# Six pairs of row blocks instead of four take seven products in the second matmul of a feed-forward beside a long convolution, with their factors in tiles that fall idle

## The chip, the cores and the metric

One Trainium2 chip, of which the kernel uses one core. The metric is the device time of one execution in microseconds (us); the time before is the median of three runs. TensorE (PE in the profile) multiplies matrices, VectorE (DVE) and ScalarE (ACT) work element by element, GpSimd (POOL) and SyncE (SP) issue DMAs here. Each engine executes its own instructions in the order in which they stand in the program, and waits where one of them needs what another engine has not yet made.

## The reference

```python
def _A_ref(q, k, v, shift_k, ssm_k, ssm_D):
    # k_shift: causal depthwise convolution of k with 4 taps
    kv = k_shift * v
    # kv_f, kf_f: FFT over the sequence, padded to 2 S
    y = irfft2(kv_f * kf_f)[:S]
    y = y + kv * ssm_D
    return q * y

def _B_ref(x, w1, w2):
    h = silu(einsum("bsd,df->bsf", x, w1))
    return einsum("bsf,fd->bsd", h, w2)

x = A_q                       # (1, 2048, 1024)
xn = _layernorm(x)
return x + _A_ref(xn, A_k, A_v, A_shift_k, A_ssm_k, A_ssm_D) + _B_ref(xn, B_w1, B_w2)
```

S is 2048 rows, D is 1024 channels, F is 3584 hidden channels. Everything is float32.

## The kernel before

**Two pieces of work side by side.** The feed-forward (GEMM1: x times w1, a SiLU; GEMM2: h times w2) is nearly all of PE's work. The convolution runs by a split Fourier transform: eight groups of 128 channels (`g` 0 to 7; the text counts them 1 to 8), each with a gate (`kin`, `acc`: taps, times v), a split into parts (`cm`, `hl`), a first stage of 48 matmuls on PE with `cfw`, additions and products on the spectrum `spec` on DVE, a split of the result into `zh` and `zl`, an inverse of 48 matmuls with `civ` on PE, and a gated result `yt`, which is added to the output. A group's `kin`, `acc` and `spec` have one buffer each, so the groups follow one another.

**Precision.** An operand is split into a high and a low float16 part (`split`: ACT makes the high one, DVE the low one), and a product is three matmuls, high x high, high x low, low x high.

**GEMM2.** The hidden channels are 28 blocks of 128, in 14 pairs (`NP`). The rows are 16 tiles (`NT`), the output columns two halves of `W` = 512. A *plain* pair adds its two blocks to each of the 32 output tiles: 32 x 2 x 3 = 192 matmuls of 512 columns. The pairs in `PAIRS` (8, 9, 12, 13) go another way: their products for 2 x 2 blocks of rows, columns and hidden channels are formed by seven products `P1` to `P7` of sums of blocks instead of eight (`PRODUCTS` names the factor of h and the factor of w2 in each). A GEMM2 tile of that kind covers four output tiles, and there are eight of them (`tiles2`), so such a pair takes 8 x 7 x 3 = 168 matmuls, of which those of the last tile's P7 and P4 are cut into 384 and 128 columns. The price is sums: `quad` makes the seven factors of h in GEMM1 (`A11` ... `S4`), and `norms_w2` the seven factors of w2 (`B11`, `T3`, `T2`, `B21`, `T1`, `B22`, `T4`), with T2 = T3 + B11 and T4 = B21 - T2, for which a tile `hold` keeps T3 and then T2.

**Order of GEMM2.** First the plain pairs: 20 blocks in `NC` = 5 chunks of 4 for each half, whose split w2 lies in the places of `W2PLACE` (`places` are eight tiles that held x during GEMM1). Then `units2`: tile after tile, in each P1, P7, P6, P2, P5, then the next tile's P1, then P3, P4. The seven w2 factors are in the places of `FPLACE` and stay there for all eight tiles. `load_h` loads h for both parts into halves of `wo`. `evacuate2` brings a tile's sums out of PSUM with ACT and DVE, and POOL adds them to the output by DMA.

**What sets the order.** The code is a set of generators (streams) that yield operations or conditions; `Order.run` picks the stream whose next operation could start first, by a table of durations, and so writes one fixed list of instructions for each engine. A change in one stream thus moves the others. Tiles are taken from rings: `places`, `wo` (six pairs of halves), `hfs` (three), `hts` (two, `ht`: staging of h in GEMM1, and of the convolution when GEMM1 is over).

Of the kernel before, what the change touches and what calls it, by code (L numbers as in the profile page):

```python
# [20 lines left out]
P = 128  # L21
# [9 lines left out]
W = 512  # L31
# [20 lines left out]
RAWS = {"B11": [(0, 0)], "B21": [(1, 0)], "B22": [(1, 1)], "T1": [(0, 1), (0, 0)], "T2": [(0, 0)],  # L52
        "T3": [(1, 1), (0, 1)], "T4": [(1, 0)]}
# [242 lines left out]
def h3_ffn_kernel(ctx, tc, x, kp, vs, fs, shift, dskip, w1, w2, cfwd, cinv, out):  # L296
# [81 lines left out]
    hsf = [{p[0]: dram.tile([4, P, NQ, 2, P], F16, name=f"hsf{p[0]}{b}") for p in PRODUCTS.values()} for b in range(2)]  # L378
# [529 lines left out]
    def quad(i, sp):  # L908

        def factors(names, hf, toks=()):  # L910
            n = len(names)
            yield hts.ready if n == 1 else hts.pairs
            ht, ttok = (hts.tile if n == 1 else hts.pair)([P, 4 * n, 2, P], F16, n)
            yield from split(ht[:, :, 0], ht[:, :, 1], hf, wsc[:, i, 2:3], toks)
            for f, name in enumerate(names):
                yield L(hsf[sp][name][:, :, PAIRS.index(i)].rearrange("q p h s -> p q (h s)"),
                        ht[:, 4 * f:4 * f + 4].rearrange("p q h s -> p q (h s)"))
                ttok.set()
# [215 lines left out]
    def feed_forward():  # L1134
# [12 lines left out]
        for h in range(2):  # L1147
            for ts in TOGETHER[h]:
                pos = {}
                for c in range(NC):  # L1150
                    for t in ts:
# [7 lines left out]
                        yield from steps2(pos[t][0], hx, wc, c == 0, c == NC - 1)  # L1159
# [14 lines left out]
    def steps2(po, hx, wc, first, last, more=False, of=range(4), q=slice(0, W)):  # L1174
        o = po[:, q]
        for n in of:
            def mm(n=n):
                kw = dict(skip_group_check=more)
                nc.tensor.matmul(o, hx[:, n, 0, :], wc[:, n, 0, q], start=first and n == 0, stop=False, **kw)  # L1179
                nc.tensor.matmul(o, hx[:, n, 0, :], wc[:, n, 1, q], start=False, stop=False, **kw)  # L1180
                nc.tensor.matmul(o, hx[:, n, 1, :], wc[:, n, 0, q], start=False, stop=last and n == 3, **kw)  # L1181
            yield T(mm, o, [hx[:, n], wc[:, n, :, q]], 3 * (size(o) / 2400 + 0.005))
# [14 lines left out]
    def units2():  # L1197

        def product2(n, u, o, first=False, of=range(4), q=slice(0, W)):
# [7 lines left out]
            htok.set()  # L1207
            if u == len(tiles2) - 1:
# [5 lines left out]
        for u in range(len(tiles2)):  # L1214
# [18 lines left out]
            if last:  # L1233
                yield from product2("P2", u, one[0], of=(0, 1))
# [6 lines left out]
            if last:  # L1241
                yield from product2("P2", u, one[0], of=(2, 3))
# [102 lines left out]
    def load_h():  # L1345
        yield flag["factors"]
        for h in range(2):
            for c, t in [(c, t) for ts in TOGETHER[h] for c in range(NC) for t in ts]:
                yield wo.ready
                flag["h", h, t, c].what = o, _ = wo.tile([P, 4, 2, P], F16)  # L1350
                yield L(o, hs[t // 4][t % 4][:, PLAIN[4 * c]:PLAIN[4 * c] + 4])
                flag["h", h, t, c].set()
        for u, n in uses2():
            sp, q = tiles2[u]
            yield wo.ready
            flag["h2", u, n].what = o, _ = wo.tile([P, NQ, 2, P], F16)
            yield L(o, hsf[sp][PRODUCTS[n][0]][q])
            flag["h2", u, n].set()
        flag["h end"].set()
# [28 lines left out]
    def norms_w2():  # L1388
# [18 lines left out]
        for h in range(2):  # L1407
            for c in range(NC):
# [5 lines left out]
                flag["w2", h, c].n = 2  # L1414
                for a in (0, 2):
                    i = PLAIN[4 * c + a] // 2
                    raw, tok = yield from next_w2()
                    add(split(wc[:, a:a + 2, 0, :], wc[:, a:a + 2, 1, :], raw, tau[:, i:i + 1], (tok, flag["w2", h, c])), 0.05)
        yield places[FPLACE[0]].ready
        hold, ktok = places[FPLACE[0]].tile([P, NQ, W], F32)  # L1420
        for k, (name, (_, of)) in enumerate(PRODUCTS.items()):
            r = places[FPLACE[k + 1]]
            yield r.ready
            wc, wtok = w2f[name] = r.tile([P, NQ, 2, W], F16)
            flag["w2f", name].n = NQ
            held = of in ("T2", "T3", "T4")
            if held:
                if of != "T3":
                    yield flag["held", before]
                flag["held", of].n = NQ  # L1430
                before = of
            for a, i in enumerate(PAIRS):
                raw, tok = yield from next_w2()
                src, toks = raw, (tok, flag["w2f", name])
                if held:
                    src, toks = hold[:, a], (flag["w2f", name], flag["held", of])
                if of == "T3":
                    b12, t12 = yield from next_w2()
                    yield v_tt(src, raw, b12, SUB)
                    tok.set()  # L1440
                    t12.set()
                elif of == "T2":
                    yield v_tt(src, src, raw, ADD)
                    tok.set()
                elif of == "T4":
                    yield v_tt(src, raw, src, SUB)
                    tok.set()
                elif of == "T1":
                    b11, t11 = yield from next_w2()
                    yield v_tt(raw, raw, b11, SUB)  # L1450
                    t11.set()
                add(split(wc[:, a, 0, :], wc[:, a, 1, :], src, tau2[:, i:i + 1], toks), 0.05)
        yield flag["held", "T4"]
        ktok.set()
# [8 lines left out]
    def load_w2():  # L1463
# [4 lines left out]
        for h, j in [(h, j) for h in range(2) for j in PLAIN[::2]]:  # L1468
# [4 lines left out]
        for _, of in PRODUCTS.values():  # L1473
            for i in PAIRS:
                for q, h in RAWS[of]:
                    yield lambda: free("ready")
                    raw, tok = free("ready")[0].tile([P, W])
                    yield L(raw, w2r[:, 2 * i + q, h * W:(h + 1) * W])
# [20 lines left out]
    def convolution(floor):  # L1499
# [13 lines left out]
        ctxs["nm"] = ps_r  # L1513
# [491 lines left out]
```

## Time and profile before

| | |
|---|---|
| three runs | 1236.89, 1237.17, 1238.01 us |
| median | 1237.17 us |
| profiled execution, first to last instruction (its span) | 1235.0 us |
| PE busy | 1225.7 us, 99% of the span |
| DVE busy | 1121.9 us, 91% |
| ACT busy | 744.0 us, 60% |
| POOL busy | 142.0 us, 12% |
| HBM traffic | 236 GB/s over the span |

The profile gives the span of one execution; its time with what lies around the span isn't listed, and the median of the runs is 2.2 us longer than the span. A row of a group reads: line, engine, operation, output <- inputs, shapes, count | busy us, mean ns of one | idle us of the engine just before, and what ended it. A row in order of time begins with its start and its length in us. Matmuls overlap in the pipeline, so their mean (377 ns for 512 columns) is more than the distance from one to the next. In the rows by stage "PEclk" is the granted clock of PE as a share of its full speed.

### The profile page before, as it was taken

What the parts mean: (1) busy time and instruction counts of PE and PEld (TensorE: products, weight loads), DVE (VectorE), ACT (ScalarE), POOL (GpSimd) and SP (SyncE); (2) the same over time, 40 slices, a digit from 0 to 9 for tenths busy, and PEclk for the clock granted to TensorE, in tenths of its full rate; (3) what the DMA queues carried; (4) which work ended last, traced back from release to release, by engine and by line L of the source; (5) the groups of instructions that cost most, each with busy time, mean ns of one, the idle gap of its engine ahead of it and who ended that gap; (6) DMA issues with size and microseconds to landing.
All of it is one profiled execution on the core that took longest, in us unless ns stands there. A gap on an engine that the chain in (4) does not pass through costs nothing.

```text
span 1235.0 us, 17269 instructions
## 1 busy us (share of the span) xinstructions
PE 1225.7 (99%) x6128; PEld 596.6 (48%) x6128; DVE 1121.9 (91%) x1366; ACT 744.0 (60%) x1299; POOL 142.0 (12%) x164
## 2 busy tenths in 40 slices
PE   9999999999999999999999999999999999999998
PEld 7645444444444444444444544544454454445445
DVE  8999996989699979998999899989979979998993
ACT  7778887877767787758653632563263264536231
POOL 2000000000000020001110300210030030113114
PEclk9999999999999999999999999999999999999999
DMA  9289889999999698968997887699596688978777
GB/s 341 78 278 312 304 298 308 286 273 335 324 359 286 218 303 278 268 213 242 345 336 184 190 257 179 155 271 259 115 216 171 134 167 247 255 161 137 164 147 103
DMA packets 254438, 293.21 MB, mean 237 GB/s; under 512 B 48784, under 2 KB 167824, under 8 KB 252176
## 3 DMA queue, kind: packets, MB, share of 16 engines
q1 hardware_dynamic: 227760, 267.46, 69.3%
q0 software_dynamic: 26592, 24.65, 15.1%
q8 instruction: 48, 0.79, 0.3%
q14 instruction: 38, 0.31, 0.1%
HBM read 193.48 MB, written 98.57 MB: 236 GB/s over the span
## 4 chain that ended last, share of the span: by engine, by line
PE 96%; DVE 2%; ACT 1%; issue 1%; DMA 1%; POOL 0%; DVEq 0%
PE ff L1179 15%; PE ff L1180 15%; PE ff L1181 15%; PE ff L1027 13%; PE ff L1028 13%; PE ff L1029 13%; PE ps L1668 2%; PE ps L1669 2%; PE ps L1670 2%; PE ft L616 1%; PE ps L1863 1%; PE ps L1861 1%; PE ps L1862 1%; DMA out<-yt 1%; PE ff L1932 1%
## 5 line engine op out<-in xcount | busy, mean ns | idle before, releaser
L1180 PE MATMUL ff<-x,wo 128*128 128x512 f16 (+2 forms) x872 | 328.5, 377 | 0.0
L1179 PE MATMUL ff<-x,wo 128*128 128x512 f16 (+2 forms) x872 | 328.4, 377 | 0.0
L1181 PE MATMUL ff<-x,wo 128*128 128x512 f16 (+2 forms) x872 | 328.4, 377 | 0.0
L1028 PE MATMUL ff<-x,wo 128*128 128x512 f16 (+2 forms) x840 | 306.7, 367 | 1.5 <-DVE x L351 1.5
L1027 PE MATMUL ff<-x,wo 128*128 128x512 f16 (+2 forms) x840 | 306.7, 367 | 0.2 <-ACT hf L359 0.2
L1029 PE MATMUL ff<-x,wo 128*128 128x512 f16 (+2 forms) x840 | 306.7, 367 | 0.1
L348 DVE TENSOR_TENSOR spec<-spec 128x1024 f32<-128x1024 f32 (+2 forms) x272 | 263.0, 999 | 2.4
L1181 PEld LDWEIGHTS <-wo 128*128 128x128 f16 x872 | 85.3, 98 | 101.5
L1179 PEld LDWEIGHTS <-wo 128*128 128x128 f16 x872 | 85.3, 98 | 100.7
L1180 PEld LDWEIGHTS <-wo 128*128 128x128 f16 x872 | 85.3, 98 | 99.4
L1029 PEld LDWEIGHTS <-wo 128*128 128x128 f16 x840 | 82.1, 98 | 92.3 <-issue 1.6
L1027 PEld LDWEIGHTS <-wo 128*128 128x128 f16 x840 | 82.1, 98 | 88.1
L1028 PEld LDWEIGHTS <-wo 128*128 128x128 f16 x840 | 82.1, 98 | 86.9 <-issue 0.5
L345 POOL DMA_DIRECT2D out<-hf x59 | 52.5, 890 | 445.0 <-ACT hf L359 341.8
L359 ACT ACTIVATE hf<-ff,invc 128x512 f32<-128x512 f32 x60 | 41.0, 684 | 101.4 <-PE ff L1181 81.8
L345 POOL DMA_DIRECT2D out<-yt x56 | 62.0, 1278 | 326.4 <-DVE yt L351 186.7
L348 DVE TENSOR_TENSOR tmp<-spec 128x2048 f32<-128x2048 f32 (+1 forms) x48 | 92.3, 1932 | 0.9
L351 DVE SCALAR_TENSOR_TENSOR ht<-hf,wsc,ht 128x1024 f16<-128x1024 f32 (+1 forms) x56 | 67.4, 1203 | 14.5 <-ACT ht L359 14.0
L351 DVE SCALAR_TENSOR_TENSOR acc<-kin,taps,acc 128x1024 f32<-128x1024 f32 x48 | 61.4, 1278 | 7.3 <-ACT acc L359 7.3
L359 ACT ACTIVATE spec<-ps 128x512 f32<-128x512 f32 x96 | 55.4, 591 | 19.9 <-PE ps L1670 18.6
L359 ACT ACTIVATE spec<-spec 128x1024 bf16<-128x1024 f32 x32 | 33.7, 1054 | 54.9 <-DVE spec L348 54.9
L351 DVE SCALAR_TENSOR_TENSOR wo<-raw,wsc,wo 128x512 f16<-128x512 f32 (+1 forms) x56 | 56.4, 1011 | 8.3 <-ACT wo L359 8.1
(183 smaller groups left out, 1751.1 us busy)
## 6 DMA issues: line engine op xcount, KB each, us to landing
wo<-hs SPq DMA_DIRECT2D x160, 256.0 KB, 3.6
hs<-ht SPq DMA_DIRECT2D x80, 256.0 KB, 4.5
wraw<-in_w SPq DMA_DIRECT2D x31, 512.0 KB, 5.4
out<-hf POOLq DMA_DIRECT2D x59, 256.0 KB, 4.5
raw<-in_w SPq DMA_DIRECT2D x28, 512.0 KB, 5.8
kin<-in_kp SPq DMA_DIRECT2D x16, 704.0 KB, 6.2
kf<-in_fs SPq DMA_DIRECT2D x8, 1024.0 KB, 5.9
hl<-in_vs SPq DMA_DIRECT2D x32, 256.0 KB, 6.1
```

The source lines that it names most:

```text
L345: return Op("POOL", 1.1, 4.8, lambda: nc.gpsimd.dma_start(o, i, accum_op=ADD), [i], [o], m, n)
L348: return V(lambda: nc.vector.tensor_tensor(o, a, b, op=op), o, [a, b], **k)
L351: return V(lambda: nc.vector.scalar_tensor_tensor(o, a, s, b, op0=op0, op1=op1), o, [a, b] + ([] if isinstance(s, float) else [s]), **k)
L359: nc.scalar.activation(o, i, func, scale=scale, **kw)
L1027: nc.tensor.matmul(o, w[:, 0, k], xf[:, :, k, 0], start=first and k == 0, stop=False, **kw)
L1028: nc.tensor.matmul(o, w[:, 0, k], xf[:, :, k, 1], start=False, stop=False, **kw)
L1029: nc.tensor.matmul(o, w[:, 1, k], xf[:, :, k, 0], start=False, stop=last and k == KH - 1, **kw)
L1179: nc.tensor.matmul(o, hx[:, n, 0, :], wc[:, n, 0, q], start=first and n == 0, stop=False, **kw)
L1180: nc.tensor.matmul(o, hx[:, n, 0, :], wc[:, n, 1, q], start=False, stop=False, **kw)
L1181: nc.tensor.matmul(o, hx[:, n, 1, :], wc[:, n, 0, q], start=False, stop=last and n == 3, **kw)
L1668: nc.tensor.matmul(o, cf[:, 0], hi[i], start=i == 0, stop=False, **kw)
L1669: nc.tensor.matmul(o, cf[:, 0], lo[i], start=False, stop=False, **kw)
```

## The change

Pairs 4 and 5 (`MORE`) join the pairs that take seven products, for which their h is made into factors in GEMM1 and their w2 into factors before GEMM2's second part. The plain part then has 16 blocks: four chunks in each half, each with a place of its own. The factors of the four pairs of before (`MAIN`) go to seven places, and those of the two new pairs elsewhere (`HOMES`): those of P1 and P7 in place 7, that of P6 in the convolution's `kin` tile once the last group has left it, those of P2 and P5 in its `acc` tile likewise, those of P3 and P4 in the two pairs of `hts` once the convolution has allotted its last group's tiles (`conv tail`). `hold` goes: T3 and T2 are written to DRAM (`summed`) and loaded again for T2 and T4. In a product of GEMM2 the four main pairs come first, then the two new ones; their h is loaded for two products at a time (`hsx`).

```diff
-PAIRS = (8, 9, 12, 13)
-NQ = len(PAIRS)
-PLAIN = [j for j in range(NF) if j // 2 not in PAIRS]
-NC = len(PLAIN) // 4
-W2PLACE = [(2, 7, 6, 3, 4), (0, 1, 5, 2, 7)]
-FPLACE = (6, 3, 4, 0, 1, 5, 2, 7)
+MAIN = (8, 9, 12, 13)
+MORE = (4, 5)
+PAIRS = MAIN + MORE
+NM, NE, NQ = len(MAIN), len(MORE), len(PAIRS)
+CHUNKS = [(0, 4), (4, 4), (12, 4), (20, 4)]
+NC = len(CHUNKS)
+W2PLACE = [(2, 7, 6, 3), (0, 1, 5, 4)]
+FPLACE = (2, 6, 3, 0, 1, 5, 4)
+HOMES = ((7, 2), ("kin", 1), ("acc", 2), ("hts", 1), ("hts", 1))
...
-        def product2(n, u, o, first=False, of=range(4), q=slice(0, W)):
+        def product2(n, u, o, first=False, of=(0, NQ), q=slice(0, W)):
+            k, f = BATCH[n]
...
-            yield from steps2(o, hx, wc, first, True, not first, of, q)
-            if 3 not in of or q.stop < W:
+            both = [(hx[:, a], wc[:, a]) for a in range(NM)][slice(*of)]
+            end = of[1] == NQ
+            yield from steps2(o, both, first, False, not first, q)
+            if end:
+                yield flag["h2x", u, k]
+                xx, xtok = flag["h2x", u, k].what
+                yield flag["w2x", n]
+                both = [(xx[:, f, a], w2x[n][:, a]) for a in range(NE)]
+                yield from steps2(o, both, False, True, not first, q)
...
+        homes, left = list(HOMES), []
         for k, (name, (_, of)) in enumerate(PRODUCTS.items()):
-            r = places[FPLACE[k + 1]]
+            r = places[FPLACE[k]]
             yield r.ready
-            wc, wtok = w2f[name] = r.tile([P, NQ, 2, W], F16)
...
+            wc, wtok = w2f[name] = r.tile([P, NM, 2, W], F16)
+            flag["w2f", name].n, flag["w2x", name].n = NM, NE
             for a, i in enumerate(PAIRS):
+                if i == MORE[0]:
+                    if not left:
+                        left = yield from home(*homes.pop(0))
+                    w2x[name] = wc = left.pop(0)
+                a = a % NM
+                done = flag["w2f" if i in MAIN else "w2x", name]
                 raw, tok = yield from next_w2()
...
+                if len(RAWS[of]) > 1:
+                    other, otok = yield from next_w2()
+                    yield v_tt(raw, raw, other, ADD if of == "T2" else SUB)
+                    otok.set()
+                add(split(wc[:, a, 0, :], wc[:, a, 1, :], raw, tau2[:, i:i + 1], (tok, done)), 0.05)
+                if of in ("T3", "T2"):
+                    yield L(summed[of, i], raw)
...
+    def home(where, n):
+        shape = [P, n, NE, 2, W]
+        if where == "hts":
+            yield lambda: flag["conv tail"]() and hts.pairs()
+            t, _ = hts.pair(shape, F16)
+        elif where in ("kin", "acc"):
+            yield flag["last", where]
+            r = ctxs[where]
+            yield r.ready
...
```

The changed kernel has some 15 lines more at its head, so its GEMM2 matmuls are L1194 to L1196 (before L1179 to L1181), its inverse matmuls L1916 to L1918 (L1861 to L1863), its sums L354 (L348) and its DVE splits L357 (L351). Three places of the order follow. `ff` are PSUM banks of the feed-forward, `ps` those of the convolution, `x` the places, `wo` halves with h or, late, with a result.

PE, around the last inverse matmul of the convolution. Before, with 218 of PE's 11,963 rows behind this piece's fourth row:

```order
L1862 MATMUL ps_10349<-zl_10329,civ 128x2x128
L1863 LDWEIGHTS civ
L1863 MATMUL ps_10349<-zh_10315,civ 128x2x128
L1179 LDWEIGHTS wo_194
L1179 MATMUL ff_10191<-x_9237,wo_194 128x512
L1180 LDWEIGHTS wo_194
```

and now, with 1,849 of 11,891 behind the fourth row, where `ht_219` holds P3's factors of the two new pairs for tile 0:

```order
L1917 MATMUL ps_9446<-zl_9428,civ 128x2x128
L1918 LDWEIGHTS civ
L1918 MATMUL ps_9446<-zh_9420,civ 128x2x128
L1194 LDWEIGHTS wo_215
L1194 MATMUL ff_8568<-ht_219,wo_215 128x512
L1195 LDWEIGHTS wo_215
```

The last convolution matmul has moved from the last tile of GEMM2's second part to the first.

DVE, from the third of the last group's four `zl` pieces on. Before:

```order
L351 SCALAR_TENSOR_TENSOR zl_10309<-spec,csc_8805,ht_200 128x1024
L351 SCALAR_TENSOR_TENSOR wo_195<-ps_10282,csc_8805,ht_199 128x512
L351 SCALAR_TENSOR_TENSOR zl_10329<-spec,csc_8805,zh_10315 128x1024
L351 SCALAR_TENSOR_TENSOR wo_194<-ps_10308,csc_8805,ht_200 128x512
L351 SCALAR_TENSOR_TENSOR wo_191<-ps_10328,csc_8805,xg_9672 128x512
L351 SCALAR_TENSOR_TENSOR hf_196<-ff_10191,invc_156,hf_196 128x512
```

and now:

```order
L357 SCALAR_TENSOR_TENSOR zl_9411<-spec,csc_8820,ht_219 128x1024
L357 SCALAR_TENSOR_TENSOR yt_3175<-ps_9395,csc_8820,ht_220 128x512
L357 SCALAR_TENSOR_TENSOR zl_9428<-spec,csc_8820,zh_9420 128x1024
L357 SCALAR_TENSOR_TENSOR yt_3175<-ps_9410,csc_8820,ht_219 128x512
L354 TENSOR_TENSOR wraw_3176<-wraw_3176 128x512
L357 SCALAR_TENSOR_TENSOR ht_219<-hf_216,tau_175,ht_219 128x512
L357 SCALAR_TENSOR_TENSOR ht_219<-hf_218,tau_175,ht_219 128x512
L357 SCALAR_TENSOR_TENSOR ht_220<-ps_9427,csc_8820,xg_9133 128x512
```

The splits of P3's new factors, and after them those of all of P4's, stand behind the convolution's last `zl`, and the evacuations of the product tiles (`hf<-ff`) behind those; before, the last w2 factor stood 91 rows ahead of that `zl`.

DVE, where the last group's `kin` and `acc` are in use for the last time, now:

```order
L357 SCALAR_TENSOR_TENSOR acc<-kin,taps,acc 128x1024
L354 TENSOR_TENSOR spec<-spec 128x2x2x256
L354 TENSOR_TENSOR hf_217<-hf_217,hf_218 128x512
L354 TENSOR_TENSOR acc<-acc,hl_2380 128x512
L354 TENSOR_TENSOR wraw_3176<-wraw_3176 128x512
L354 TENSOR_TENSOR acc<-acc,hl_2380 128x512
L357 SCALAR_TENSOR_TENSOR kin<-hf_217,tau_175,kin 128x512
```

The first factor split into `kin` follows the last group's taps; P6 of tile 0 reads it.

More of the change, by code (lines that the diff above doesn't have):

```diff
@@ L1233, in units2 @@
             if last:
-                yield from product2("P2", u, one[0], of=(0, 1))
+                yield from product2("P2", u, one[0], of=(0, NM // 2))
             else:
@@ new lines, in h3_ffn_kernel @@
+    w2x = {}
+    def home(where, n):
[7 more added lines that the diff above has]
+            yield r.ready
+            t, _ = r.tile([P, T2 + HALO, P] if where == "kin" else [P, 2, T2, P])
+            t = t.rearrange("p t w -> p (t w)" if where == "kin" else "p b t w -> p (b t w)")
+            t = shaped(t[:, 0:n * NE * W], shape, F16)
+        else:
+            r = places[where]
+            yield r.ready
+            t, _ = r.tile(shape, F16)
+        return [t[:, a] for a in range(n)]
@@ L1539, in loads @@
                     flag["kin", g, b].set()
+                    if (g, b) == (NG - 1, 1):
+                        flag["last", "kin"].set()
                     if b == 0:
@@ L1568, in gate @@
                 accs[g] = acc, _ = acc_r.tile([P, 2, T2, P])
+                if g == NG - 1:
+                    flag["last", "acc"].set()
                 for a in range(2):
```

105 lines of the change are left out of this document (54 added, 51 removed).

## The prediction

> **What bounds the kernel now.** I read the page first, then what TensorE waits for, then busy time by stage, then the last 30 us in order of time.
>
> ```profile
> span 1235.0 us, 17269 instructions
> PE 1225.7 (99%) x6128; PEld 596.6 (48%) x6128; DVE 1121.9 (91%) x1366; ACT 744.0 (60%) x1299; POOL 142.0 (12%) x164
> L1180 PE MATMUL ff<-x,wo 128*128 128x512 f16 (+2 forms) x872 | 328.5, 377 | 0.0
> ```
>
> TensorE (PE) is busy for 1225.7 of 1235.0 us, VectorE (DVE) for 1121.9. L1179 to L1181 are GEMM2, 872 matmuls on each line.
>
> ```profile
> PE ff L1028 <- DVE x L351: 1.5, 1, 1.5
> PE ps L1668 <- DVE yt L351: 1.4, 1, 1.4
> ```
>
> These are the longest waits of PE (total, times, longest). PE hardly ever waits: what shortens its queue shortens the kernel, as long as nothing new makes it wait. So the question is whether DVE, at 91%, still has its results ready where the new order needs them.
>
> ```profile
> core 0: us, PE busy (x) PEld busy (x) DVE busy (x) ACT busy (x) POOL busy (x), PEclk, DMA share, GB/s
> 0.00:550.00 550.00, 547.31 (x2790) 271.94 (x2791) 498.38 (x680) 421.27 (x713) 22.27 (x41) 1.00 0.88 282
> 550.00:907.00 357.00, 354.88 (x1737) 169.24 (x1735) 334.82 (x363) 183.95 (x330) 50.53 (x51) 1.00 0.85 228
> 907.00:1210.00 303.00, 303.00 (x1481) 144.25 (x1479) 283.04 (x315) 135.41 (x253) 58.08 (x62) 1.00 0.78 177
> 1210.00:1235.00 25.00, 20.50 (x127) 11.19 (x124) 5.68 (x10) 3.33 (x5) 11.15 (x11) 0.95 0.80 116
> ```
>
> The first line names the columns; the stage's length stands ahead of them. DVE is 91 to 94% busy in every stage up to 1210 us, and it sits idle for only 51.6 + 22.2 + 20.0 = 93.8 us in all that time. Most of its work is the convolution, whose eight channel groups end like this:
>
> ```profile
> 905.68 1.28 DVE L351 SCALAR_TENSOR_TENSOR zl<-spec,csc,zh 128x1024 f16<-128x1024 f32 x1
> 1208.38 1.28 DVE L351 SCALAR_TENSOR_TENSOR zl<-spec,csc,zh 128x1024 f16<-128x1024 f32 x1
> 1212.04 0.27 PE L1863 MATMUL ps<-zh,civ 128*128 128x256 f16 x1
> 1230.28 0.22 PE L1181 MATMUL ff<-x,wo 128*128 128x128 f16 x1
> ```
>
> The last DVE piece of group 5 starts at 905.68, that of group 8 (the last) at 1208.38; the last convolution matmul follows at 1212.04, and PE's last matmul at 1230.28. So the convolution is a second, almost equally long chain that ends 18 us before PE does. It costs nothing now, because only the last part of the last GEMM2 tile stands behind it.
>
> **The change part by part.** *Fewer matmuls.* Two more pairs move from plain (32 output tiles x 2 blocks x 3 = 192 matmuls a pair) to seven products (8 tiles x 7 x 3 = 168): 2 x 24 = 48 matmuls of 512 columns less. The new order has them gone: in GEMM2, 1536 plain + 1044 in products = 2580 for 2616; the 12 more than 2616 - 48 are the last tile's pieces of 384 + 128 columns for one of 512, equal in columns.
>
> ```profile
> 1217.35 0.38 PE L1179 MATMUL ff<-x,wo 128*128 128x512 f16 x1
> 1217.57 0.38 PE L1180 MATMUL ff<-x,wo 128*128 128x512 f16 x1
> 1224.05 0.38 PE L1180 MATMUL ff<-x,wo 128*128 128x512 f16 x1
> 1214.73 0.33 PE L1179 MATMUL ff<-x,wo 128*128 128x384 f16 x1
> 1214.90 0.33 PE L1180 MATMUL ff<-x,wo 128*128 128x384 f16 x1
> 1216.68 0.22 PE L1179 MATMUL ff<-x,wo 128*128 128x128 f16 x1
> 1216.74 0.22 PE L1180 MATMUL ff<-x,wo 128*128 128x128 f16 x1
> ```
>
> Between the starts at 1217.35 and 1224.05 lie 31 matmuls, 0.216 us each; 384 columns take about 0.16, 128 about 0.055, together the same. So PE is 48 x 0.2157 = 10.4 us shorter.
>
> *More elementwise work.* Its prices, by form:
>
> ```profile
> L351 DVE SCALAR_TENSOR_TENSOR ht<-hf,wsc,ht 128x1024 f16<-128x1024 f32 x48 | 61.4, 1279 | 10.9 <-ACT ht L359 10.4 <-DMA kin<-in_kp 0.3
> L351 DVE SCALAR_TENSOR_TENSOR ht<-hf,wsc,ht 128x512 f16<-128x512 f32 x8 | 6.0, 747 | 3.7 <-ACT ht L359 3.6
> L348 DVE TENSOR_TENSOR hf<-ff,hf 128x512 f32<-128x512 f32 x52 | 35.6, 684 | 3.7 <-PE ff L1029 3.7
> L351 DVE SCALAR_TENSOR_TENSOR x<-wraw,tau,x 128x1024 f16<-128x1024 f32 x10 | 12.8, 1278 | 1.2 <-ACT x L359 1.2
> L351 DVE SCALAR_TENSOR_TENSOR x<-x,tau,x 128x512 f16<-128x512 f32 x12 | 8.8, 742 | 0.0
> L348 DVE TENSOR_TENSOR x<-hf,x 128x512 f32<-128x512 f32 x10 | 6.8, 683 | 0.1
> L351 DVE SCALAR_TENSOR_TENSOR hf<-ff,invc,hf 128x512 f32<-128x512 f32 x15 | 11.2, 744 | 5.5 <-PE ff L1181 5.5
> ```
>
> In GEMM1 a plain pair splits four tiles on DVE (4 x 1.279 = 5.1 us); as factors it splits six of that size and two halves, with eight sums (7.7 + 1.5 + 5.5 = 14.6): +9.5, for two pairs +19.0 us. In the W2 factors a pair goes from two splits (2.6) to seven halves and four sums (5.2 + 2.7 = 7.9): +5.4, for two +10.7. DVE gains 29.7 us, ScalarE about the splits' part of that, and it is at 60%. The loads and stores grow by some 50 issues on SP's queue, where the DMA share is 0.78 in the stage concerned; I cost them at nothing, covered by a DVE that is later than they are, and at up to 10 us where a load of a T4 raw is late (below).
>
> *The new wait, which decides.* A GEMM2 tile needs all seven products, so tile 0 already needs all seven new factors. Their homes are: place 7 for P1 and P7; `kin` for P6, free after its last use in group 8; `acc` for P2 and P5, free after group 8's signal parts; `ht` halves for P3 and P4, after the last group's tail has begun. Before, every factor lay in a place that the plain part had left. In the new order the last GEMM2 matmul that needs none of the late homes stands 954 us of matmul time from PE's start; from there to the first `kin` factor come only convolution matmuls of groups 6 and 7, and more than two groups of convolution are still to be done. Behind P3's `ht` factor (DVE's 1,222nd of 1,255 rows) stands nearly all of the products: after the last convolution matmul come 924 GEMM2 matmuls where it was 108. PE executes in order, so everything behind waits, until DVE has finished the convolution.
>
> So the end is: when DVE ends the convolution, plus the rest of tile 0's factors, plus seven tiles of PE, plus the tail.
>
> 1. *End of the convolution on DVE.* Up to 1210 us DVE did 498.4 + 334.8 + 283.0 = 1116.2 us of work. To the same point it now gets + 29.7, less 13 evacuations of product tiles that come after it (13 x 0.744 = 9.7), less 6 sums and 8 splits of the last factors that come after it (4.1 + 5.9 = 10.0): + 10.0. With the same 93.8 us of idle time: 1220. The other bound comes from PE's place: group 5's last inverse matmul stands behind 888.1 us of matmuls before, 895.2 now, so without new stalls group 5 ends 7 us later, at about 914; behind it are 283.0 less 9.7 and some 2 us of factor work, 271, and 20 of idle time: 1205. The order lets idle time of GEMM1 take the new work up, so I go near that: 1208.
> 2. *Rest of tile 0.* Behind the convolution's last piece DVE still has two gated results, six sums and eight splits, 1.5 + 10.0 = 11.5 us, P4's last among them; its ready time is 1208 + 11.6 = 1219.6. P3's six matmuls and most of P4's 18 lie beside it; the last three, 0.65 us, don't.
> 3. *Seven tiles.* Of the 924 matmuls, 24 are P3's and P4's; the other 900 are 864 in columns of 512: 864 x 0.2157 = 186.4 us.
> 4. *Tail.* From 1230.28 + 0.055 to 1235.0: 4.7 us, the same evacuation and stores.
>
> 1219.6 + 0.65 + 186.4 + 4.7 = 1411.4 us of span. The span of before was 1235.0 against a median of 1237.17, so 2.2 lie around it: 1413.5. Seen from PE: it would run dry at about 977 (954.2 of matmuls, and the 22.6 that PE's last end, 1230.5, lies above its 1207.9 of matmuls), and wait some 186 us in all, of which 10 are saved.
>
> One thing PE does while it waits:
>
> ```profile
> 1229.00:1230.50 1.50, 1.50 (x18) 1.05 (x15) 0.62 (x1) 0.00 (x0) 0.00 (x0) 1.00 1.09 184
> 1232.50:1233.50 1.00, 0.00 (x0) 0.00 (x0) 0.00 (x0) 0.00 (x0) 0.00 (x0) 0.57 0.19 60
> 1233.50:1235.00 1.50, 0.00 (x0) 0.00 (x0) 0.00 (x0) 0.00 (x0) 0.00 (x0) 0.50 0.00 0
> ```
>
> The granted clock is 1.00 while PE works, 0.57 in the third microsecond after its last matmul, then 0.50. A PE that waits 186 us will run its scattered convolution matmuls at half clock, and start the seven tiles so. The way back to 1.00 isn't in this trace; I take nothing for it. The Trainium skill, "TensorE: Matmul & The Clock Gate", Part 1, has the same fall to half and says that about 3.4 us of sustained work bring the full clock back; by that the restart would cost an estimated 1.7 us more and the sum be 1415.
>
> **The rivals.** *The gain comes through*: the homes come free early enough, PE never starves, and the time is 1237.2 - 10.4 = 1226.8. For this P4's last split must be done when PE gets there, at about 1011 + 23 = 1034. DVE's work before it is 1116.2 + 10.0 + 11.5 = 1138 us, which no idle time removed brings below 1138; every us that it ends after 1034 is a us of PE's wait, and the gain is used up from 1044 on. Against it speaks everything above; nothing in the profile speaks for it, since the rows of an engine stay in their order. That the matmuls aren't saved at all is excluded by the order.
>
> *DVE closes up*: freed of PE's queue, the convolution's matmuls come at once and DVE's waits vanish: 20 us less after group 5, and PE's clean pace before it, 1205 - 20 + 11.6 + 0.65 + 186.4 + 4.7 + 2.2 = 1391; with P4's factors spread among the last group's work up to 6 less, 1385. For it: in 907 to 1210 DVE waits for evacuations of PE's first stage. Against: those waits are for ScalarE behind PE and recur in each group.
>
> *Half clock on the chain*: groups 7 and 8 have 96 first-stage matmuls inside the wait; at half clock they take 96 x 0.2157 = 20.7 us longer, and if DVE waits for all of it the time is 1434; with the equal-idle bound of 1220 too, 1446. Against: before, the first stage of a group was spread over 36 us of PE's queue with other work between, so even 20.7 us fits into what DVE is used to.
>
> **How the numbers follow.** The forecast, 1413.5 give or take 12 us, 0.6; DVE closes up, 0.18; half clock on the chain or equal idle, 0.18; the gain comes through, 0.01; a wait that I have misread and that cancels the gain to within 0.2% (about what a measurement here tells from no change), 0.01; the rest in 0.02 is still slower. Range 1385 to 1445: the two rivals that end slower. Faster 0.01, same 0.01, slower 0.98.
>
> **What would show it.** In the profile after: PE busy for about 1215 us of a span of about 1411; PE's waits led by the factor splits in `kin`, `acc` and `ht` and by the convolution's first stage, about 180 us; slices of PE at 2 or 3 tenths with a low clock from about 980 to 1215, then seven tiles without a gap while DVE is at 1 tenth; GEMM2's matmul count 860 on each line; DVE about 1150 busy. I am wrong if PE reaches the second tile before DVE has done group 8's last `zl`, if the stretch behind that piece is far from 200 us, or if DVE ends group 8 far from 1208.

## The result, and the profile after

| | before | after |
|---|---|---|
| runs | 5 | 5 |
| median | 1236.89 us | 1440.46 us |
| lowest to highest | 1235.37 to 1238.01 | 1437.18 to 1444.82 |
| profiled execution (its span) | 1237.17 (1235.0) | 1444.82 (1443.0) |

The changed kernel takes 1.165 times as long (95% interval 1.1628 to 1.1672). The forecast was 1413.5 us. Its profiled execution is the slowest of its five runs, 4.4 us above their median; sums against the trace below use its span of 1443.0 us.

The page of the changed kernel: span, busy time, and three rows of the span in 40 slices of 36 us.

```profile
span 1443.0 us, 17352 instructions
...
PE 1243.9 (86%) x6091; PEld 597.4 (41%) x6092; DVE 1150.2 (80%) x1408; ACT 755.2 (52%) x1317; POOL 142.0 (10%) x164
...
PE   9999999999999999999999999995422702599999
...
DVE  8999998878996999979989999899799999200001
...
PEclk9999999999999999999999999998755855699999
```

PE works at nine tenths through slice 27 (to about 974 us) and again from slice 36 (about 1262 us). Between them it waits while DVE goes on nearly as before; then seven tiles run without a gap, with DVE at nothing. The clock row falls in the same slices. PE's longest waits (total, times, longest):

```profile
PE ps L474 <- ACT spec L365: 62.1, 4, 43.2
PE ff L1194 <- ACT kin L365: 23.5, 1, 23.5
PE ff L1194 <- ACT acc L365: 22.7, 1, 22.7
PE ff L1194 <- ACT x L365: 20.6, 5, 10.8
PE ps L1721 <- ACT tmp L365: 19.5, 2, 14.8
PE ps L1916 <- ACT zh L365: 13.7, 2, 13.3
```

66.8 us of them are waits for late w2 factors (`kin`, `acc`, and `x` for those of the main pairs); the other 95.3 are waits for steps of the convolution, where `L474` is a tiny matmul over sums of one of its tiles. Both have one origin: PE has nothing left in its queue but the convolution's chain and what stands behind it. Busy time by stage, in the columns of the prediction, and ahead of them the same up to and from group 5's last `zl`; the last row is the split of this stretch before the change:

```profile
0.00:929.06 929.06, 910.46 (x4546) 443.08 (x4548) 852.24 (x1075) 615.54 (x1058) 77.81 (x98) 1.00 0.88 264
929.06:1221.14 292.08, 132.48 (x601) 62.23 (x599) 272.04 (x297) 110.77 (x216) 31.41 (x32) 0.70 0.43 101
0.00:550.00 550.00, 540.65 (x2750) 267.95 (x2752) 498.97 (x684) 422.86 (x708) 22.26 (x41) 1.00 0.90 286
1175.00:1200.00 25.00, 0.00 (x0) 0.00 (x0) 24.38 (x25) 4.24 (x7) 0.00 (x0) 0.50 0.00 0
1275.00:1300.00 25.00, 25.00 (x117) 11.37 (x116) 1.50 (x2) 3.33 (x5) 3.44 (x4) 1.00 0.61 135
```

```profile
0.00:905.68 905.68, 900.87 (x4514) 440.04 (x4515) 831.91 (x1041) 604.62 (x1040) 72.46 (x92) 1.00 0.87 261
905.68:1208.38 302.70, 302.70 (x1480) 144.19 (x1478) 282.70 (x316) 136.01 (x254) 57.17 (x61) 1.00 0.79 178
```

The first fence is the kernel after, the second the kernel before. Up to group 5's end DVE does 852.24 us of work for 831.91, 20.3 more, and needs 23.4 us longer: it sits idle for 76.8 us, before for 73.8. From there to group 8 it is 20.0 us idle in both. At 1175 to 1200 PE does nothing and DVE is 98% busy; at 1275 to 1300 it is the other way round.

DVE's last pieces, in order of time (start, length, in brackets the idle time before and what ended it):

```profile
929.06 1.28 DVE L357 SCALAR_TENSOR_TENSOR zl<-spec,csc,zh 128x1024 f16<-128x1024 f32 x1
...
1221.14 1.29 DVE L357 SCALAR_TENSOR_TENSOR zl<-spec,csc,zh 128x1024 f16<-128x1024 f32 x1 [0.61 <-issue]
...
1228.93 0.69 DVE L354 TENSOR_TENSOR wraw<-wraw,hf 128x512 f32<-128x512 f32 x1 [1.93 <-DMA hf<-sumT]
...
1241.38 0.69 DVE L354 TENSOR_TENSOR wraw<-wraw,hf 128x512 f32<-128x512 f32 x1 [10.22 <-DMA hf<-sumT]
...
1249.56 0.75 DVE L357 SCALAR_TENSOR_TENSOR ht<-wraw,tau,ht 128x512 f16<-128x512 f32 x1 [0.79 <-ACT ht L365]
```

The convolution's last piece starts at 1221.14 (before at 1208.38). P4's last factor, on which seven tiles hang, follows only 28 us later, 10 of which pass in waiting for one load.

### The profile page after: what moved, and what is told of

Its sections match the earlier page's. It is cut to its first block, busy times and chain, and to the rows that moved or that the text cites. A ratio compares the mean times of both kernels' runs of the same rounds, so it can differ in the third digit from the quotient of the medians.

```text
span 1443.0 us, 17352 instructions
## 1 busy us (share of the span) xinstructions
PE 1243.9 (86%) x6091; PEld 597.4 (41%) x6092; DVE 1150.2 (80%) x1408; ACT 755.2 (52%) x1317; POOL 142.0 (10%) x164
## 4 chain that ended last, share of the span: by engine, by line
PE 55%; DVE 21%; issue 12%; DMA 7%; ACT 3%; POOL 1%; SPq 0%; DVEq 0%; POOLq 0%; ACTq 0%
PE ff L1041 10%; PE ff L1043 10%; PE ff L1042 10%; DVE spec L354 9%; PE ff L1195 7%; PE ff L1196 7%; PE ff L1194 7%; DVE tmp L354 4%; DMA out<-yt 2%; DVE acc L357 2%; DVE spec L357 2%; DMA wraw<-in_w 1%; POOL out L351 1%; DVE x L357 1%; PE ps L1721 1%
## 5 line engine op out<-in xcount | busy, mean ns | idle before, releaser
L1194 PE MATMUL ff<-x,wo 128*128 128x512 f16 x778 | 295.2, 380 | 20.6 <-ACT x L365 20.6
L1041 PE MATMUL ff<-x,wo 128*128 128x512 f16 (+2 forms) x840 | 307.3, 368 | 5.2 <-DVE hf L354 4.1
L1042 PE MATMUL ff<-x,wo 128*128 128x512 f16 (+2 forms) x840 | 307.3, 367 | 1.4 <-DVE x L357 1.4
L1043 PE MATMUL ff<-x,wo 128*128 128x512 f16 (+2 forms) x840 | 307.5, 368 | 0.7 <-DVE wo L357 0.7
L1195 PE MATMUL ff<-x,wo 128*128 128x512 f16 x778 | 295.4, 380 | 9.7 <-DVE x L357 9.7
L1196 PE MATMUL ff<-x,wo 128*128 128x512 f16 x778 | 295.8, 381 | 0.0
L354 DVE TENSOR_TENSOR spec<-spec 128x1024 f32<-128x1024 f32 (+2 forms) x272 | 264.5, 999 | 1.9
L357 DVE SCALAR_TENSOR_TENSOR hf<-ff,invc,hf 128x512 f32<-128x512 f32 (+2 forms) x19 | 13.1, 694 | 177.1 <-ACT hf L365 108.0
L1196 PEld LDWEIGHTS <-wo 128*128 128x128 f16 x860 | 84.7, 98 | 117.5 <-issue 20.9
L1194 PEld LDWEIGHTS <-wo 128*128 128x128 f16 x860 | 85.0, 99 | 113.6 <-issue 17.3
L351 POOL DMA_DIRECT2D out<-yt x60 | 67.1, 1307 | 466.7 <-DVE yt L357 332.7
L351 POOL DMA_DIRECT2D out<-hf x61 | 53.5, 886 | 502.0 <-ACT hf L365 389.6
L354 DVE TENSOR_TENSOR tmp<-spec 128x2048 f32<-128x2048 f32 (+1 forms) x48 | 92.3, 1932 | 0.8
L357 DVE SCALAR_TENSOR_TENSOR ht<-hf,wsc,ht 128x1024 f16<-128x1024 f32 (+1 forms) x56 | 65.2, 1164 | 9.0 <-ACT ht L365 8.8
L1721 PE MATMUL ps<-hl,cfw 128*128 128x512 f16 x122 | 48.1, 395 | 24.7 <-ACT tmp L365 19.5
```

Source lines behind the costliest of these rows:

```text
L351: return Op("POOL", 1.1, 4.8, lambda: nc.gpsimd.dma_start(o, i, accum_op=ADD), [i], [o], m, n)
L354: return V(lambda: nc.vector.tensor_tensor(o, a, b, op=op), o, [a, b], **k)
L357: return V(lambda: nc.vector.scalar_tensor_tensor(o, a, s, b, op0=op0, op1=op1), o, [a, b] + ([] if isinstance(s, float) else [s]), **k)
L1041: nc.tensor.matmul(o, w[:, 0, k], xf[:, :, k, 0], start=first and k == 0, stop=False, **kw)
L1042: nc.tensor.matmul(o, w[:, 0, k], xf[:, :, k, 1], start=False, stop=False, **kw)
L1043: nc.tensor.matmul(o, w[:, 1, k], xf[:, :, k, 0], start=False, stop=last and k == KH - 1, **kw)
```

## Experiments

Each run is compared with runs of the kernel before on the same chip, medians 1236.95, 1237.16 and 1238.34 us in the three rounds. In the reading of most stands where DVE's last `zl` started, with the busy time up to it (in the order PE, PEld, DVE, as above).

**e3: the 48 matmuls alone.** On the kernel before, no new factors:

```diff
-PLAIN = [j for j in range(NF) if j // 2 not in PAIRS]
+PLAIN = [j for j in range(NF) if j // 2 not in PAIRS + (4, 5)]
-W2PLACE = [(2, 7, 6, 3, 4), (0, 1, 5, 2, 7)]
+W2PLACE = [(2, 7, 6, 3), (0, 1, 5, 2)]
...
+        m = of.index(3) if twice and 3 in of else None
+        for k, n in enumerate(of if m is None else of[:m] + [0, 1] + of[m:]):
```

> The kernel before with only the matmuls of the change: the plain part has 16 blocks, and in each of the seven products two pairs are multiplied twice, so GEMM2 has 48 matmuls of 512 columns less, while GEMM1 makes no new factors; the w2 splits of pairs 4 and 5 (5 us on DVE) fall out too. Both theories: PE has 10.4 us less, the convolution ends as before at about 1205, and the time is 1227. Were it 1233 or more, then the end of the convolution on DVE would already bound the kernel before, and the whole idea could not gain its 10.4 us.

1226.01 us, ratio 0.9911 (0.9896 to 0.9926): 10.9 us less for the 10.4 forecast, so the prediction's price of a matmul holds. (This kernel multiplies the same factors twice and so leaves out products that the output needs.)

```profile
0.00:1201.42 1201.42, 1195.00 (x5971) 580.38 (x5973) 1109.74 (x1353) 735.51 (x1292) 132.67 (x156) 1.00 0.82 233
```

**e2: the new factors of h in GEMM1 alone.** On the kernel before; GEMM2 keeps its form:

```diff
+MORE = (4, 5)
+QUADS = PAIRS + MORE
-        if i in PAIRS:
+        if i in QUADS:
...
+                to = hsf[sp][name][:, :, PAIRS.index(i)] if i in PAIRS else hsx[sp][name][:, :, MORE.index(i)]
...
+                j = PLAIN[4 * (c if c != 2 else 1)]
```

> The kernel before with one part of the change: in GEMM1 pairs 4 and 5 are made into seven factors of h (19 us more on DVE) and stored, but GEMM2 is as before and reads the blocks of pairs 2 and 3 a second time for those of 4 and 5. Theory A (the added elementwise work fits into DVE's idle time): 1237 to 1240. Theory B (it delays the convolution almost one for one): its last piece starts at 1220 to 1227 instead of 1208 and the time is 1245 to 1256.

1252.64 us, ratio 1.0127 (1.0109 to 1.0146): 15.7 us more.

```profile
0.00:1230.25 1230.25, 1216.48 (x6047) 589.22 (x6049) 1133.40 (x1380) 748.86 (x1305) 132.24 (x156) 1.00 0.85 239
```

DVE has 18.8 us more work up to the last `zl` than before (1133.4 for 1114.6), close to the 19.0 that the prediction priced, and the piece comes 21.9 us later. The 96.8 us of idle time took nothing up. PE is idle for 13.8 us up to the piece (before 4.8), and the kernel ends 19 us behind it, where it was 27. I take it from these numbers that the end of DVE's chain now decides. Theory B's time holds; its piece comes 3 us later than expected.

**e1: no late homes.** On the kernel after:

```diff
-                yield flag["w2x", n]
-                both = [(xx[:, f, a], w2x[n][:, a]) for a in range(NE)]
+                early = n if n in ("P1", "P7") else "P1"
+                yield flag["w2x", early]
+                both = [(xx[:, f, a], w2x[early][:, a]) for a in range(NE)]
...
+                if i in MAIN or k < 2:
                     add(split(wc[:, a, 0, :], wc[:, a, 1, :], raw, tau2[:, i:i + 1], (tok, done)), 0.05)
+                else:
+                    tok.set()
```

> The changed kernel without the late homes: the w2 factors of pairs 4 and 5 are made for P1 and P7 only (place 7); PE reads P1's for the other five products, whose raw w2 is still loaded, summed and stored, but not split (10 splits on DVE and ACT, 7.4 us each, left out). Theory A (the wait for homes that the convolution frees is the whole loss): PE no longer runs dry, and the time is 1237 - 10.4 = 1227, up to 1232 with the tail. Theory B (DVE is a second bound, almost as long as PE; the 29.7 us of elementwise work were not absorbed by its idle time, since DVE idled 51.0 us of the first 550 after and 51.6 before): the homes cost most of the 203 us, but the convolution's last piece still starts at about 1222 or later instead of 1208, and the last tile behind it ends at 1240 to 1250, no gain.

1265.91 us, ratio 1.0225 (1.0197 to 1.0253). Nearly 175 us of the loss falls away with the wait, but the kernel is 29 us slower than before, above both expectations.

```profile
0.00:1246.26 1246.26, 1209.63 (x5985) 585.14 (x5987) 1135.10 (x1388) 746.23 (x1305) 131.55 (x154) 0.99 0.85 242
```

The last `zl` is 37.9 us later than before, with 20.5 us more work on DVE. The other 17.4 are new idle time, whose cause I haven't found.

**e6: the whole change with homes set aside early.** On the kernel after: two pairs of `hts`, two of `wo` and one of `hfs` are taken before the plain part ends, and the convolution can no longer use spare `hts` tiles.

```diff
-HOMES = ((7, 2), ("kin", 1), ("acc", 2), ("hts", 1), ("hts", 1))
+HOMES = ((7, 2), ("hts", 1), ("wo", 1), ("hts", 1), ("wo", 1), ("hfs", 1))
...
+    def keep_homes():
+        yield flag["activations"]
+        for where, r in (("hts", hts), ("hts", hts), ("hfs", hfs)):
+            yield r.pairs
+            kept_at[where].append(r.pair([P, 1, NE, 2, W], F16)[0])
...
-                yield lambda: r.ready() or flag["activations"]() and hts.ready()
+                yield lambda: r.ready() or False
```

> The changed kernel in full, with other homes: the two pairs of ht halves, two pairs of wo and one of hf are set aside when GEMM1 is over, so no factor waits for the convolution; the convolution loses ht as spare, the loads of h have 8 halves for 12, and raw w2 may use hf when one pair is free. Theory A: 1227 to 1235, the change gains once no factor waits for the convolution. Theory B: the wait of 180 us is gone, but DVE's end of the convolution, at 1225 or later, bounds: 1240 to 1255.

1261.53 us, ratio 1.0191 (1.0174 to 1.0208): all the arithmetic of the change, without its great wait, and 24.6 us slower than before. This is above both expectations.

```profile
0.00:1238.86 1238.86, 1207.01 (x5972) 582.38 (x5974) 1142.36 (x1400) 747.20 (x1306) 133.46 (x156) 0.98 0.86 243
```

DVE has 27.8 us more work up to the last `zl`, which is 30.5 us later; idle 96.5 for 93.8. PE is idle for 31.8 us in this time (before 4.8), with this as its longest wait:

```profile
1011.98 0.63 PE L1736 MATMUL ps<-hl,cfw 128*128 128x512 f16 x1
1019.28 0.16 PE L474 MATMUL ps<-css,oneb 128*128 128x4 bf16 x1 [6.67 <-ACT spec L365]
1019.31 0.59 PE L1194 MATMUL ff<-x,wo 128*128 128x512 f16 x1
1019.69 0.63 PE L1195 MATMUL ff<-x,wo 128*128 128x512 f16 x1
1020.12 0.63 PE L1196 MATMUL ff<-x,wo 128*128 128x512 f16 x1
```

A step of the convolution comes later than its place in PE's queue. GEMM2 matmuls that need nothing of it stand behind it, wait too, and then start 0.43 us apart for the usual 0.216, as those ahead of this wait already did, behind one of 3.9 us. Against e3, which has the same 6091 matmuls, the span is 39.2 us longer: PE is idle for 36.6 us for 9.4, and busy for 1226.8 us for 1214.8.

**e10: the late wait alone.** On the kernel before, P4's factors are held back until the convolution's last split:

```diff
+            if name == "P4":
+                yield flag["conv end"]
...
+                    if (g, t) == (NG - 1, TO[-1]):
+                        flag["conv end"].set()
```

> The kernel before with the wait alone: P4's factors of w2 are made only when the convolution's last piece has been split; no other work is added or taken away. Theory A (in-order PE stands still until then, and nearly all product tiles come behind): the last piece starts at 1198 to 1208 (13 evacuations, 10 us, now come behind it), P4's four sums and eight... four splits take some 8 to 12 us more, then 588 matmuls of 512 columns, 126.8 us, and 4.7 of tail: 1335 to 1355. Rival E (the late homes only showed a loss that the added work makes anyway): 1237 to 1260.

1337.52 us, ratio 1.0807 (1.0791 to 1.0823): 99 us from one wait, with not one instruction of arithmetic more or less. Theory A's range holds. The last `zl` starts at 1197.31, P4's last split ends at 1205.2, and the span ends 129.9 us after that. PE's longest waits:

```profile
PE ps L464 <- ACT spec L359: 59.2, 2, 49.2
PE ps L1670 <- ACT tmp L359: 14.9, 1, 14.9
PE ps L1865 <- ACT zh L359: 13.3, 1, 13.3
```

They have the names of after's waits for the convolution, and nearly the same longest ones: 49.2, 14.9 and 13.3 us for 43.2, 14.8 and 13.3.

**e5: another place for the last raws.** On the kernel after, the last raw blocks of w2 may also lie in `hl`, once the convolution has left it:

```diff
-            return [r for r in (ctxs["wraw"], hfs)[:1 + rest] if getattr(r, kind)()]
+            two = [ctxs["wraw"], hfs][:1 + rest] + [ctxs["hl"]] * flag["parts end"]()
+            return [r for r in two if getattr(r, kind)()]
```

> The changed kernel, where the raw w2 of the last factors may also be loaded into the convolution's hl tiles once the last group has its parts. In the profile after, P4's factors were ready at 1250 instead of the 1220 that the prediction's sum had, 28 us behind the convolution's last piece for 11.6; DVE waited 13 us there for loads of the stored sums, and the load waited 10 us for an hf half whose result GpSimd had not yet sent, behind the convolution's last stores. Theory: with other buffers that wait goes, P4 is ready 10 to 15 us earlier, 1426 to 1431. Rival (the loads' and ScalarE's own latency makes the 28 us): 1437 to 1444.

1434.5 us, ratio 1.1604 (1.158 to 1.1629), between the two expectations.

```profile
1236.03 0.75 DVE L357 SCALAR_TENSOR_TENSOR ht<-hl,tau,ht 128x512 f16<-128x512 f32 x1 [5.92 <-DMA out<-ht]
```

P4's last split now starts at 1236.03, not 1249.56. The spans of the two profiles differ by 13.4 us, but one is of the fastest run of its kernel and the other of the slowest; by the medians the gain is 6.0, and the times of the two kernels overlap (1431.41 to 1439.6 here). Of the 13.5 us, 3.7 are the convolution's own earlier end (its last `zl` starts at 1217.42 here), so 9.8 belong to the loads. What is left of the wait is for GpSimd's store of an `ht` tile, which is to hold the factor.

**e4: one pair instead of two**, on the kernel after, with `MORE = (4,)` and homes in place 7 and three halves of `wo`.

```diff
-MORE = (4, 5)
+MORE = (4,)
-CHUNKS = [(0, 4), (4, 4), (12, 4), (20, 4)]
+CHUNKS = [(0, 4), (4, 4), (10, 2), (12, 4), (20, 4)]
-HOMES = ((7, 2), ("kin", 1), ("acc", 2), ("hts", 1), ("hts", 1))
+HOMES = ((7, 4), ("wo", 1), ("wo", 1), ("wo", 1))
```

> One pair more (pair 4) instead of two, homes in place 7 and three halves of wo, all sums on DVE as in the change. Theory B: DVE's work grows by 14.9 us, the convolution's last piece starts at about 1223, and the end comes some 20 to 25 us later: 1243 to 1248, half of the loss of two pairs with early homes. Theory A (elementwise work fits into DVE's idle time): 1232.

1260.46 us, ratio 1.0184 (1.0169 to 1.0199). This is above both expectations. DVE's last `zl` starts at 1217.98, 5 us earlier than expected, yet the end lies 40 us behind it. Here DVE's end no longer sets the time; PE does, having waited 24.7 us up to there and run slowly behind its waits, of which this is the longest:

```profile
1064.17 0.17 PE L474 MATMUL ps<-css,oneb 128*128 128x6 bf16 x1 [8.17 <-ACT hl L365]
1064.20 0.59 PE L1194 MATMUL ff<-x,wo 128*128 128x512 f16 x1
1064.58 0.63 PE L1195 MATMUL ff<-x,wo 128*128 128x512 f16 x1
```

**e7 and e8: GEMM1's new sums on GpSimd.** e7 is e6, e8 is e4, each with the four sums of `quad` moved from DVE:

```diff
-        yield v_tt(v, z, v, ADD)
-        yield v_tt(z, x, z, SUB)
+        yield p_tt(v, z, v, ADD)
+        yield p_tt(z, x, z, SUB)
```

> The early homes again, in full, with the 48 sums that make the factors of h in GEMM1 (4 for each of 6 pairs and 2 row halves) moved from DVE to GpSimd: 48 x 0.684 = 32.8 us off DVE, which then has about 3 us less than in the kernel before. Theory B (DVE's convolution chain is the second bound, and its added work is what costs the 25 us with early homes): the convolution's last piece starts at about 1206 to 1212 for 1239, PE bounds again, and the 10.4 us come through: 1227 to 1232. Rival C (GpSimd's sums are slow or slow DVE down, or the homes taken from ht, wo and hf are what costs): the time stays above 1240.

> One pair more (pair 4) instead of two, with its seven new factors in place 7 and three halves of wo, and the 40 sums of GEMM1's factors on GpSimd. Theory B: 24 matmuls of 512 columns less (5.2 us), DVE 14.9 us more for the pair and 27.4 less for the sums: 1232. Rival C: above 1240.

e7: 1288.47 us, ratio 1.0415 (1.0396 to 1.0434). e8: 1288.02 us, ratio 1.0411 (1.0393 to 1.043). Rival C's bound holds in both. They are 27 and 28 us slower than e6 and e4, with the sums on DVE. Groups of e7:

```profile
L357 POOL TENSOR_TENSOR hf<-x,hf 128x512 f32<-128x512 f32 x12 | 23.5, 1961 | 0.9
L354 DVE TENSOR_TENSOR spec<-spec 128x1024 f32<-128x1024 f32 x136 | 172.3, 1278 | 0.8
```

and the latter in e6:

```profile
L354 DVE TENSOR_TENSOR spec<-spec 128x1024 f32<-128x1024 f32 x136 | 164.5, 1218 | 0.8
```

In the means of its four groups a sum of 128x512 takes GpSimd 1.6 to 2.0 us (0.684 on DVE). DVE's own sums of the spectrum became 5% longer on the average, and its busy time is 1152.9 us against 1148.2 in e6, though 32.8 us of work left it. The last `zl` starts 12.2 us later than in e6 (1251.05); what makes up the rest of the 27 us these runs don't part.

**e9: GEMM1's sums left out** of e6.

```diff
-        yield v_tt(v, z, v, ADD)
-        yield v_tt(z, x, z, SUB)
```

> The early homes again, with the 48 sums of GEMM1's factors left out altogether (the factors are split from the plain blocks, so h's sums are missing in the output): 32.8 us off DVE and nothing put on GpSimd. So far DVE's idle time up to the convolution's last piece was 92 to 97 us in every kernel without GpSimd sums, whatever its work, the kernel before included. Theory B (that end is DVE's work plus this idle time): the last piece starts at 1239 - 33 = 1206, PE is the bound again, and the time is 1227 to 1235. Rival D (the homes taken from ht, wo and hf are what costs the 25 us): 1250 or more, with the last piece at 1206 all the same or idle time grown.

1247.89 us, ratio 1.0078 (1.006 to 1.0096), between the expectations.

```profile
0.00:1214.63 1214.63, 1192.68 (x5909) 576.62 (x5911) 1112.12 (x1351) 746.99 (x1305) 131.84 (x154) 0.99 0.86 246
```

With 30.2 us less work than in e6 the last `zl` comes 24.2 us earlier. The kernel ends 32.5 us behind it and stays 10 us slower than before, since PE has waited 22.0 us up to there.

## Why the prediction came out as it did

**What was right.** PE runs out of work, waits for the convolution and the late factors, and runs seven tiles after all else; 860 matmuls on each line of GEMM2; DVE busy 1150 us. 0.65 + 186.4 + 4.7 is 191.75 us; from the end of P4's last split, 1249.56 + 0.75 = 1250.3, to the end of the span it is 192.7. e10 shows the wait without the change's arithmetic, and e1 and e6 the change without the wait.

**What was wrong: 31.6 us of the span.** The forecast gave 1413.5 us, give or take 12, a chance of 0.6; the measured 1440.5 lies 27 us above it, where two rivals were to end. Two of the signs of being wrong came at least in part: behind the last `zl` lie 221.9 us, not 200, and group 8 ends 14 us late. The terms of the sum, in us of the profiled execution:

| step | forecast | measured | off |
|---|---|---|---|
| 1: end of the convolution on DVE | 1208 | 1221.14 + 1.29 = 1222.4 | 14.4 |
| 2: rest of tile 0's factors | 11.6 | 1250.3 - 1222.4 = 27.9 | 16.3 |
| 3 and 4: seven tiles, tail | 191.8 | 192.7 | 0.9 |

*Step 1 failed where it chose between its bounds:* "The order lets idle time of GEMM1 take the new work up, so I go near that: 1208." It took none up. In the first 550 us DVE did 498.97 us of work, before 498.38, so the new work pushed the old back. DVE's work up to the last `zl` was 9.7 us more than before (10.0 in the working), with 96.9 us of idle time for 93.8; the bound "with the same 93.8 us of idle time: 1220" was the right one. The other bound took group 5's place in PE's queue as its time, but group 5's last `zl` ended at 930.3 (929.06 + 1.28), not 914. PE's idle time up to there is 18.6 us, where it was 4.8, and the waits listed in it are for results of DVE and ScalarE. The mistake lies in reading PE's 99% as the whole pace. I read DVE's idle time as waits inside a chain of its own, which recur with each step; what supports this is its size. In eight of the twelve profiles (before, after, e2 to e6 and e10) it is 91 to 97 us up to the last `zl`, while DVE's work up to there runs from 1103 to 1142. In e9 it is 102.5, in e1 111.2, and in e7 and e8, with sums on GpSimd, 104.9 and 103.5.

*Step 2 failed at the loads.* The working counted DVE's 11.6 us of instructions and put the loads at nothing, "up to 10 us where a load of a T4 raw is late (below)"; nothing below took the 10 in. SP's and GpSimd's issues in order of time:

```profile
1226.79 0.55 SPq L338 DMA_DIRECT2D wo<-hsfS  x1
1237.47 0.32 SPq L338 DMA_DIRECT2D hf<-sumT  x1
```

```profile
1229.55 1.08 POOL L351 DMA_DIRECT2D out<-ht  x1 [2.38 <-issue]
1233.40 0.88 POOL L351 DMA_DIRECT2D out<-hf  x1 [2.77 <-DMA out<-ht]
```

The load of a stored sum for P4 (`sumT`) goes into a half of `hfs` whose last content is a result that GpSimd has still to store, behind the convolution's stores. SP issues nothing between 1226.79 and 1237.47. DVE's wait of 10.22 us above is this one. With `hl` as another place (e5) the loads take 9.8 us less in the profiles, and 6.0 us of the medians go.

*The clock* made PE busy for 1243.9 us, not 1215 (e3, with the same matmuls, has 1214.8): 29 us of matmuls at half speed. Nearly all lie inside the wait, as "half clock on the chain" said, but that rival's price is not paid: DVE's idle time after group 5 is 20.0 us, as before. That the time fell among those that it gave, 1434 to 1446, is chance: of its two parts only the equal idle time came true, and the late loads happen to make up for the other. "DVE closes up" fails by the same number, since its 20 us did not vanish. The restart, which the sum took at nothing, costs about 2 us:

```profile
1250.37 0.58 PE L1195 MATMUL ff<-ht,wo 128*128 128x512 f16 x1 [0.20 <-DVE ht L357]
1250.74 0.63 PE L1196 MATMUL ff<-ht,wo 128*128 128x512 f16 x1
...
1254.58 0.63 PE L1196 MATMUL ff<-x,wo 128*128 128x512 f16 x1
...
1255.36 0.38 PE L1195 MATMUL ff<-x,wo 128*128 128x512 f16 x1
```

PE works without a gap from 1250.37, and only at about 1255.2 do the starts come 0.216 us apart instead of 0.43. So the full clock took 4.8 us to return, nearly half of it lost. The Trainium skill, "TensorE: Matmul & The Clock Gate", Part 1, speaks of at least one busy window of about 3.4 us, which runs freely; the direction agrees, and the measured return is longer than one such window. In the table's last row a shorter tail hides most of this cost: PE's last matmul starts at 1439.71, so 3.2 us lie behind it where the sum had 4.7.

**Where 203.6 us come from**, by medians: the matmuls saved give back 10.9 (e3). GEMM1's factors alone cost 15.7 (e2). All of the change with early homes in place of the late ones is 24.6 slower than before (e6). The late homes cost the other 179 against that version (1440.5 - 1261.5), of which 6 are the load that waits for GpSimd's store (e5). So the rival "the gain comes through" falls twice: its homes don't come early, and with early homes there is no gain either. Part of that second loss is shown: the new factors of h alone cost more (15.7) than the matmuls give back (10.9), since the convolution's chain on DVE ended only 27 us before the kernel did and gets 18.8 us more work from them.

**Open.** The rest of e6's loss isn't explained by DVE's work: without the sums DVE has 2.5 us less of it up to the last `zl` than before the change, and the kernel is still 10 us slower than before (e9). Whether that comes from the tiles that its homes take from `ht`, `wo` and `hf`, or from an order whose convolution steps stand too early in PE's queue, these runs don't part; nor do they explain e1's 17.4 us of idle time. A version that beats the kernel before was not found.

## What to carry to other kernels

A trade of PE time for DVE time is worth what the second chain leaves over, not what the busy shares leave over: look for where the other engine's chain ends, add the new work one to one, and count its idle time as part of the chain unless a row shows a wait that the change removes. (Here e2, e6 and the change itself came out so to about 3 us; e1 did not.) In an engine that executes in order, a buffer that comes free late stops everything that stands behind its first use, so ask of each new buffer when its last user leaves and what stands in the queue behind. Count for the load of a late operand also the store that must first leave its buffer.

## What the runs showed of the hardware that I had not expected

GpSimd's sums hold up instructions of DVE, and only those of a certain kind. Taking 48 sums of 128x512 from DVE to GpSimd gave DVE back nothing (1148.2 to 1152.9 us). Two moments of e7 show why; first DVE, then GpSimd, in order of time:

```profile
318.22 0.69 DVE L354 TENSOR_TENSOR spec<-spec,ps 128x512 f32<-128x512 f32 x1 [0.54 <-ACT spec L370]
...
419.42 1.75 DVE L354 TENSOR_TENSOR spec<-spec 128x512 f32<-128x512 f32 x1
```

```profile
318.22 1.27 POOL L357 TENSOR_TENSOR hf<-x,hf 128x512 f32<-128x512 f32 x1
...
419.03 1.59 POOL L357 TENSOR_TENSOR x<-x 128x512 f32<-128x512 f32 x1
```

Where one input of DVE's sum lies in PSUM (`ps`), it takes 0.69 us beside a sum on GpSimd, as it does alone, and GpSimd's takes 1.27. Where both inputs lie in SBUF and GpSimd's sum has begun, DVE's takes 1.75 us, longer by about as much as GpSimd still needs. Of the 19 sums of DVE in e7 that have both inputs in SBUF and begin inside one of those 48, 18 take 0.8 to 1.1 us longer than alone; of the six with an input in `ps`, none does. All of DVE's instructions that begin inside them take 34.4 us more together than alone, about the 32.8 that were moved. The Trainium skill, "GPSIMD Engine Reference", section 1, has GpSimd's access to SBUF shared with VectorE, with contention for VectorE instructions of two SBUF inputs. The rows agree.

A wait in the middle of PE's queue can cost more than its length: in e4 the matmuls ahead of the wait of 8.17 us start 0.216 us apart and those behind it 0.43, with a granted clock of 0.50 from 1064 to 1068 us.
